# Turning the key-value sums of a linear attention: four TensorE transpositions and a copy, or one VectorE transposition and eight DMA moves

## The chip, the cores and the metric

The kernel runs on one core of a Trainium2 chip. A core has five engines that run their own instruction lists side by side: TensorE (PE in the profile, with its weight loads shown as PEld), VectorE (DVE), ScalarE (ACT), GpSimd (POOL) and SyncE (SP). SP computes nothing here; it issues DMAs, one after the other, and waits where a DMA has to wait. The metric is the device time of one execution in microseconds (us).

## The reference

Two branches are computed from the same input `x` (2048 rows of 512) and mixed row by row with a gate `g`:

```python
qkv = x @ wqkv                              # 32 heads of 16
pq, pk = q @ w_phi, k @ w_phi               # per head
phi = concat(softmax(p), softmax(-p))       # 32 features per head, for q and for k
kv = sum over rows s of phi_k[s]^T v[s]     # per head 32 x 16
z  = sum over rows s of phi_k[s]            # per head 32
a = (phi_q @ kv) / (phi_q . z + 1e-6) @ wo
b = mish(x @ w1 + b1) @ w2                  # 512 -> 1376 -> 512
out = g * a + (1 - g) * b,  g = sigmoid(x . gate_w)
```

`kv` is a sum over all 2048 rows, so no numerator `phi_q @ kv` can be made before the whole key pass is over.

## The kernel before, in words

The kernel has two passes. Pass A runs over eight chunks of 256 rows: it projects k, v and q (each fp32 product is made from three TensorE products of a high and a low part), turns k into features and adds `phi_k^T v` into one PSUM tile `kvp`, which lives through the whole pass. Pass B runs over four blocks of 512 rows: eleven steps `up0` to `up10` make the hidden columns of branch b, `dn0` to `dn10` multiply them by `w2`, and between them stand the q features, the numerators `nu0` and `nu1` (PE reads `kvb`, the turned kv sums, as weights, and `eT`, the turned q features, as the moving side), and the products `wo0` to `wo3` with `wo`.

The order of everything is written out by hand in the strings `FIRST` to `BLOCK`: each word names a step, `run` carries the steps out in that order, and `pin` keeps every instruction in it. So each engine's queue is the order of the words that give it work. A word with `+` belongs to the next stage.

The steps around the change:

- `km` is the last word of `LAST`, the last chunk of pass A. VectorE multiplies `kvp` by a mask of zeros and ones (`mask`, made by GpSimd at the start of the kernel at L193) and writes the result to an SBUF tile `km` (L455). `kvp` holds sums for pairs of heads, and the mask keeps only products of a head with itself.
- `@kt` stands in `BLOCK0` after `up3` and ahead of `dn1`. PE makes four 128x128 transpositions of `km` against the identity `ident` into a PSUM tile `kvT` (L460), and ScalarE copies that to `kvb` (issued at L461, recorded under the helper's line L121). `kvT` takes one of the three PSUM buffers of the tag `a`, which the `up` tiles use in turn.
- `mi3`, `hi3` and `lo3` follow `@kt` in the string: ScalarE's Mish of `up3`, its rounding `h`, and GpSimd's remainder `l` (L504).
- `gr` in `BLOCK0` sends the gate's row out and back (L531, L532), `lq3` loads q rows (L553), `mv0` and `mv1` move the turned q features to `eT` with sixteen DMAs each (L592). All of these are in SP's queue. `mv0` waits for `tr1`, a VectorE transposition (L572).
- `nu0` in `BLOCK0`, after `dn5`, is the first reader of `kvb` (L602, recorded under L101).

VectorE's transposition (the profile calls it STREAM_TRANSPOSE) turns each 32x32 block by itself: the blocks stay where they are.

Of the kernel before, what the change touches and what calls it, by code (L numbers as in the profile page):

```python
# [8 lines left out]

F32 = mybir.dt.float32  # L10
# [5 lines left out]
P = 128  # L16
# [5 lines left out]
NG = 4  # L22
SC = 256
# [37 lines left out]

BLOCK0 = """
    up0 mi0 hi0 lo0 gr lq3 S1 rS1 mx2 mn2 d02 d12 up1 @z mi1 hi1 lo1 T0 D0 m0 de0 rd0 sc0 es0 tr0 up2 mi2 hi2 lo2 dn0
    T1 D1 m1 de1 rd1 sc1 es1 tr1 mv0 lq0+ lq1+ mx3 mn3 d03 d13 up3 @kt mi3 hi3 lo3 dn1
    up4 mi4 hi4 lo4 WL0 dn2 E2 S2 T2 rS2 D2 m2 de2 rd2 sc2 es2 tr2 up5 mi5 hi5 lo5 WL1 dn3 E3 ge gg up6 mi6 hi6 lo6 dn4
    up7 mi7 hi7 lo7 dn5 nu0 oh0 S3 T3 rS3 ol0 D3 m3 de3 rd3 sc3 es3 tr3 mv1 up8 mi8 hi8 lo8 dn6
    mx0+ mn0+ d00+ d10+ mx1+ mn1+ d01+ d11+ lq2+ lq3+ wo0 ag0 wo1 ag1 E0+ E1+ S0+ T0+ rS0+ D0+ m0+ de0+ rd0+ sc0+ es0+ tr0+
# [22 lines left out]
def tile_gated_mix(ctx: ExitStack, tc: tile.TileContext, xT, wv, wkT, wqT, bd, w1a, w1b, b1, w2a, w2b, wo, out):  # L90
    nc = tc.nc
    const = ctx.enter_context(tc.tile_pool(name="const", bufs=1))
# [4 lines left out]
    pin = tc.keep_in_program_order  # L97
    V, G_, A_, Sy = nc.vector, nc.gpsimd, nc.scalar, nc.sync

    def mm(*a, **k):  # L100
        return pin(nc.tensor.matmul(*a, **k))  # L101

    def T(shape, dt, tag, bufs, name):
        nm[0] += 1
        return sp.tile(shape, dt, name=f"{name}_{nm[0]}", tag=tag, bufs=bufs)

    def k8(name, tag, dt=F32R):
        return T([P, 2048], dt, tag, 2 if tag in ("eT", "E") else 1, name)

    def k4(name, tag, dt=F32):  # L110
        return T([P, 1024], dt, tag, {"tx": 2, "oh": 2, "z": 1}[tag], name)

    def k2(name, tag, dt=F32):
        return T([P, 512], dt, tag, {"pq": 3, "io": 4, "hl": 8}[tag], name)

    def psum(name, tag, bufs={"a": 3, "dn": 4, "kv": 1}):
        nm[0] += 1
        return pp.tile([P, 512], F32, name=f"{name}_{nm[0]}", tag=tag, bufs=bufs[tag])

    def act(out_, in_, fn=AF.Copy, **k):  # L120
        return pin(A_.activation(out_, in_, fn, **k))  # L121
# [7 lines left out]
    def f32(ap):  # L129
        return ap.bitcast(F32)  # L130
# [52 lines left out]
    md = k2("md", "io")[:, :P].rearrange("p (h f) -> p h f", f=DH)  # L183
# [2 lines left out]
    pin(G_.affine_select(md, md, pattern=[[DH, 8], [0, DH]], compare_op=ALU.is_ge, fill=0.0, base=DH - 1, channel_multiplier=-1))  # L186
    b1s = const.tile([P, NF], F32, name="b1s")
    pin(G_.dma_start(b1s, b1))
    ident = const.tile([P, P], F32, name="ident")
    make_identity(nc, ident)  # L190
    mask = const.tile([P, 2, 2, 32], F32, name="mask")
    for a in range(2):
        pin(G_.tensor_add(mask[:, :, a, :], *[md[:, o : o + 4, :].rearrange("p (r h) f -> p r (h f)", r=2) for o in (0, 4)]))  # L193
    g_sb = const.tile([P, S // P], F32, name="g_sb")
    og_sb = const.tile([P, S // P], F32, name="og_sb")
    ge_sb = const.tile([P, S // P], F32, name="ge_sb")
    kvb = const.tile([P, NG, P], F32, name="kvb")


    steps = {}  # L200
# [1 line left out]
    def at(key, name, fn):  # L202
        steps.setdefault((key, name), []).append(fn)
# [11 lines left out]
    kvs = []  # L215
# [226 lines left out]
    B = {}  # L442

    def mid_ops():
        key = ("A", NCH - 1)

        def zh():
            B["zs"] = [k4("zs", "tx", F32R) for _ in range(2)]
            act(B["zs"][0], zacc)

        def km():
            B["km"] = k2("km", "io")
            shape = [P, NG, 2, 64]
            m = mask[:, :, :, :].rearrange("p r a f -> p r (a f)")[:, None, :, :].to_broadcast(shape)
            pin(V.tensor_mul(B["km"][:, :].rearrange("p (g r f) -> p g r f", g=NG, r=2), kvs[0][:, :, None, :].to_broadcast(shape), m))  # L455

        def kt_():
            pt = psum("kvT", "a")
            for G in range(NG):
                pin(nc.tensor.transpose(pt[:, G * P : (G + 1) * P], B["km"][:, G * P : (G + 1) * P], ident))  # L460
            act(kvb, pt[:, :].rearrange("p (g d) -> p g d", g=NG))  # L461

        def z():
            B["zb"] = k4("zb", "z")
            for a in range(2):
                ps = psum("z", "dn")
                for j in range(2):
                    mm(ps, onr, B["zs"][j][:, a * 512 : (a + 1) * 512], start=(j == 0), stop=(j == 1))
                act(B["zb"][:, a * 512 : (a + 1) * 512], ps)

        at(key, "zh", zh)
        at(key, "zl", lambda: pin(V.tensor_sub(B["zs"][1], zacc, f32(B["zs"][0]))))
        at(key, "km", km)
        at(("B", 0), "@kt", kt_)
        at(("B", 0), "@z", z)


    def b_ops(b):
# [68 lines left out]
        for t in range(4):  # L547
            d = {}
# [37 lines left out]
        for h in range(2):  # L586
            def mv(h=h):
                eTs[h] = k8("eT", "eT", F32)[:, :].rearrange("p (t q x) -> p t q x", t=2, q=4)
                for q in range(4):
                    for k in range(4):  # L590
                        o = 64 * (k % 2) + 32 * (k // 2)
                        pin(Sy.dma_start(eTs[h][o : o + 32, :, q, :], Ep[key, h][32 * q : 32 * q + 32, :, k * 256 : (k + 1) * 256]))  # L592

            def nu(h=h):
                ev = eTs[h][:, :, :, :].rearrange("p t q (b c) -> p b (t q) c", c=32)
                po = [psum("num", tag) for tag in (("a", "a") if b and h else ("kv", "a"))]
                for bh in range(2):
                    for c in range(4):
                        u = 4 * bh + c
                        for r in range(2):  # L600
                            o = (u % 2) * 64 + 32 * r
                            mm(po[r][32 * c : 32 * c + 32, bh * SC : (bh + 1) * SC], kvb[64 * r : 64 * r + 64, u // 2, o : o + 32], ev[64 * r : 64 * r + 64, u, :, :], start=True, stop=True, skip_group_check=True)  # L602
                for r in range(2):
                    num[h, r] = po[r]

            def oh(h=h):
                for gp in range(2):
                    ohl[h, gp] = k4("ohl", "oh", F32R)
                    act(ohl[h, gp][:, :512], num[h, gp])

            def ol(h=h):
                for gp in range(2):
                    pin(V.tensor_sub(ohl[h, gp][:, 512:], num[h, gp], f32(ohl[h, gp][:, :512])))

            at(key, f"mv{h}", mv)
            at(key, f"nu{h}", nu)
            at(key, f"oh{h}", oh)
            at(key, f"ol{h}", ol)
# [56 lines left out]
    x_ops(0, (("A", NCH - 2), "ldx", "ldw0"), ("A", NCH - 1))  # L675
    wo_ops()
    mid_ops()
    for b in range(NB):
        b_ops(b)
# [47 lines left out]
    for j in range(2):  # L727
        h, l = [w[:, 2 * j : 2 * j + 2, :].rearrange("p k f -> p (k f)") for w in (wvh, wvl)]
# [94 lines left out]
```

## Time and profile before

| what | value |
|---|---|
| median of 3 runs | 450.24 us (450.02 to 450.66) |
| the profiled execution | 449.89 us, of which 448.2 us span from its first to its last instruction |
| TensorE busy | 443.4 us, 99% of the span |
| VectorE busy | 307.6 us, 69% |
| ScalarE busy | 194.6 us, 43% |
| GpSimd busy | 164.7 us, 37% |
| mean granted TensorE clock | 0.999 of full speed |

The span is what the profile shows of the program; the rest of the profiled execution's time, 1.7 us, lies before and after it. All views are of that one execution. A row of the timeline gives the start in us from the span's start, the duration in us, the engine, the line of the kernel, the operation, the tiles written and read, the shape and the number of instructions merged into the row; in square brackets stands how long the engine stood idle before it, and what ended that. A row of the chain that ended last gives the start, how much of the span the piece takes up, and what it is. Matmul records overlap, because PE starts a matmul before the one ahead of it has drained; the distance between starts is what a matmul costs PE.

### The profile page before, as it was taken

How to read it: one execution, taken by the hardware profiler on the slowest of the kernel's cores; microseconds unless marked ns; L12 is line 12 of the kernel's file. 1: busy time of each engine (PE TensorE's matmuls, PEld its weight loads, DVE VectorE, ACT ScalarE, POOL GpSimd, SP SyncE). 2: the span in 40 equal slices, each digit the busy share in tenths (PEclk: the TensorE clock that was granted, in tenths of full speed). 3: DMA queues.
4: the chain of work that ended last, by engine and by line, in shares of the span. 5: the costliest groups of instructions: out<-in, count | busy, mean ns of one | idle time of the engine just before them, and what ended most of it. 6: DMA issues, size and time to landing. Idle time of an engine off the chain costs nothing.

```text
span 448.2 us, 7216 instructions
## 1 busy us (share of the span) xinstructions
PE 443.4 (99%) x2882; PEld 363.9 (81%) x2882; DVE 307.6 (69%) x411; ACT 194.6 (43%) x268; POOL 164.7 (37%) x102
## 2 busy tenths in 40 slices
PE   8999999999999999999999999999999999999996
PEld 7888888888888888878788878888878888887885
DVE  3798559459398999997979998369769329701103
ACT  3644533444335465627255352644262643242330
POOL 3448687677861445521122220214220222221121
PEclk9999999999999999999999999999999999999999
DMA  7721522614623100405243151321241302030002
GB/s 264 278 95 47 191 68 97 191 12 175 188 81 111 48 24 20 123 17 143 78 112 123 40 151 53 89 95 47 60 129 48 94 1 95 18 78 1 1 0 95
DMA packets 26026, 40.09 MB, mean 89 GB/s; under 512 B 5764, under 2 KB 14468, under 8 KB 25992
## 3 DMA queue, kind: packets, MB, share of 16 engines
q1 hardware_dynamic: 25672, 39.22, 28.6%
q8 instruction: 23, 0.38, 0.3%
q10 hardware_dynamic: 288, 0.39, 0.2%
q14 instruction: 11, 0.09, 0.1%
q0 software_dynamic: 32, 0.01, 0.0%
HBM read 22.82 MB, written 8.40 MB: 70 GB/s over the span
## 4 chain that ended last, share of the span: by engine, by line
PE 99%; ACT 0%; DVE 0%; issue 0%
PE proj L101 30%; PE up L101 27%; PE down L101 27%; PE wo L101 10%; PE kvp L101 2%; PE num L101 2%; PE fuse L101 1%; PE warm L101 1%; PE rest L101 0%; PE z L101 0%; ACT wkh L121 0%; DVE io L654 0%; PE kvT L460 0%; DVE ones L171 0%
## 5 line engine op out<-in xcount | busy, mean ns | idle before, releaser
L504 POOL TENSOR_TENSOR l<-act,h 128x512 fp32r<-128x512 f32 x44 | 63.9, 1453 | 218.0 <-ACT h L121 183.8
L121 ACT ACTIVATE act<-up,b1s 128x512 f32<-128x512 f32 x44 | 30.3, 689 | 92.2 <-PE up L101 91.3
L324 POOL TENSOR_TENSOR zacc<-zacc,E 128x1024 f32<-128x1024 f32 x16 | 39.8, 2486 | 43.9 <-DVE E L286 43.9
L121 ACT ACTIVATE E<-E 128x1024 f32<-128x1024 f32 x32 | 33.4, 1058 | 37.3 <-DVE E L271 37.2
L286 DVE TENSOR_TENSOR E<-E,Sm 128x1024 f32<-128x1024 f32 x32 | 46.5, 1453 | 1.1
L275 DVE TENSOR_REDUCE Sm<-E 128x64 f32<-128x1024 f32 x32 | 38.6, 1206 | 5.0 <-ACT E L121 5.0
L101 PE MATMUL wo<-woh,ohl 128*128 128x512 f32 x128 | 41.2, 389 | 0.0
L101 PE MATMUL down<-w2ah,h 128*128 128x512 f32 x96 | 37.7, 393 | 0.0
L101 PE MATMUL down<-w2al,h 128*128 128x512 f32 x96 | 37.4, 390 | 0.0
L101 PE MATMUL down<-w2ah,l 128*128 128x512 f32 x96 | 37.4, 389 | 0.0
L259 DVE TENSOR_REDUCE mx<-proj 128x32 f32<-128x512 f32 x16 | 11.0, 689 | 32.5 <-PE proj L101 32.5
L101 PE MATMUL down<-w2bh,h 128*128 128x512 f32 x78 | 30.6, 392 | 0.0
L101 PE MATMUL down<-w2bl,h 128*128 128x512 f32 x78 | 30.4, 390 | 0.0
L101 PE MATMUL down<-w2bh,l 128*128 128x512 f32 x78 | 30.3, 389 | 0.0
L409 DVE TENSOR_TENSOR xbl<-xraw,xbh 128x1024 fp32r<-128x1024 f32 x8 | 11.9, 1526 | 26.0 <-ACT xbh L121 26.0
L121 ACT ACTIVATE h<-act 128x512 fp32r<-128x512 f32 x44 | 27.8, 632 | 1.4
L101 PEld LDWEIGHTS wo<-woh,ohl 128*128 128x128 f32 x128 | 24.0, 188 | 5.0
L121 ACT ACT_TABLE_LOAD x19 | 24.4, 1283 | 5.5 <-PE up L101 5.2
L121 ACT ACTIVATE io<-wo,g_sb 128x512 f32<-128x512 f32 x16 | 10.9, 688 | 35.2 <-PE wo L101 35.2
L101 PE MATMUL up<-xbh,w1ah 128*128 128x512 f32 x96 | 25.8, 390 | 0.0
L101 PE MATMUL up<-xbl,w1ah 128*128 128x512 f32 x96 | 25.7, 389 | 0.0
L101 PE MATMUL up<-xbh,w1al 128*128 128x512 f32 x96 | 25.7, 389 | 0.0
(123 smaller groups left out, 968.9 us busy)
## 6 DMA issues: line engine op xcount, KB each, us to landing
eT<-E SPq DMA_DIRECT2D x128, 64.0 KB, 2.0
xraw<-in_xT_dram SPq DMA_DIRECT2D x15, 512.0 KB, 4.4
pqd<-qs SPq DMA_DIRECT2D x16, 256.0 KB, 3.3
pq<-pqd SPq DMA_DIRECT2D x16, 256.0 KB, 2.9
out_dram<-io SPq DMA_DIRECT2D x15, 256.0 KB, 2.4
raw<-in_w1a_dram SPq DMA_DIRECT2D x3, 512.0 KB, 5.1
raw<-in_w2a_dram SPq DMA_DIRECT2D x3, 512.0 KB, 3.8
wT<-in_wkT_dram SPq DMA_DIRECT2D x4, 256.0 KB, 4.3
```

Source lines behind the costliest of these rows:

```text
L101: return pin(nc.tensor.matmul(*a, **k))
L121: return pin(A_.activation(out_, in_, fn, **k))
L259: pin(V.tensor_reduce(d[name], hv(src()), axis=AX.X, op=op))
L275: pin(V.tensor_reduce(d["S"], hv(d["E"][:, :]), axis=AX.X, op=ALU.add))
L286: pin(eng.tensor_mul(hv(d["E"][:, :]), hv(d["E"][:, :]), d["S"][:, :, None].to_broadcast([P, 2 * H, DH])))
L324: at(key, f"z{t}", lambda d=d: pin(G_.tensor_add(zacc, zacc, d["E"])))
L409: pin(V.tensor_sub(xb[b][1][:, :, sl], kt(raw[h], SC), f32(xb[b][0][:, :, sl])))
L504: pin(G_.tensor_sub(U[i]["l"], U[i]["a"], f32(U[i]["h"])))
```

## The change

The change alters how `km` becomes `kvb`. The multiplication by the mask now writes 256 columns rather than 512: the blocks that belong to two different halves (`r`) of a group of heads were written as zeros before, and are not written now. VectorE then turns every 32x32 block of these 256 columns in place. Eight DMAs, all in SP's queue right behind, carry the blocks to the partitions where `nu` reads them: each takes 32 partitions of 4 runs of 32 numbers, 16 KB in all. The step `@kt`, with its four transpositions, its PSUM tile and its copy on ScalarE, is gone, and so is `ident`. The mask is now 32 columns wide and made by three additions instead of two. `kvb` holds 256 columns rather than 512, and `nu` reads from it the same numbers in weights of the same shape.

```diff
-    T1 D1 m1 de1 rd1 sc1 es1 tr1 mv0 lq0+ lq1+ mx3 mn3 d03 d13 up3 @kt mi3 hi3 lo3 dn1
+    T1 D1 m1 de1 rd1 sc1 es1 tr1 mv0 lq0+ lq1+ mx3 mn3 d03 d13 up3 mi3 hi3 lo3 dn1
...
-    ident = const.tile([P, P], F32, name="ident")
-    make_identity(nc, ident)
-    mask = const.tile([P, 2, 2, 32], F32, name="mask")
-    for a in range(2):
-        pin(G_.tensor_add(mask[:, :, a, :], *[md[:, o : o + 4, :].rearrange("p (r h) f -> p r (h f)", r=2) for o in (0, 4)]))
+    mask = const.tile([P, 32], F32, name="mask")
+    for o in (2, 4, 6):
+        pin(G_.tensor_add(mask, md[:, :2, :].rearrange("p h f -> p (h f)") if o == 2 else mask, md[:, o : o + 2, :].rearrange("p h f -> p (h f)")))
...
-    kvb = const.tile([P, NG, P], F32, name="kvb")
+    kvb = const.tile([P, 8, 32], F32, name="kvb")
...
             B["km"] = k2("km", "io")
-            shape = [P, NG, 2, 64]
-            m = mask[:, :, :, :].rearrange("p r a f -> p r (a f)")[:, None, :, :].to_broadcast(shape)
-            pin(V.tensor_mul(B["km"][:, :].rearrange("p (g r f) -> p g r f", g=NG, r=2), kvs[0][:, :, None, :].to_broadcast(shape), m))
-
-        def kt_():
-            pt = psum("kvT", "a")
-            for G in range(NG):
-                pin(nc.tensor.transpose(pt[:, G * P : (G + 1) * P], B["km"][:, G * P : (G + 1) * P], ident))
-            act(kvb, pt[:, :].rearrange("p (g d) -> p g d", g=NG))
+            m = B["km"][:, :256]
+            pin(V.tensor_mul(m.rearrange("p (n x) -> p n x", x=32), kvs[0].rearrange("p g (a x) -> p (g a) x", a=2), mask[:, None, :].to_broadcast([P, 8, 32])))
+            pin(V.transpose(m, m))
+            m = m.rearrange("p (g a x) -> p g a x", g=NG, a=2)
+            for e in range(2):
+                for r in range(2):
+                    for a in range(2):
+                        o, i = 64 * r + 32 * a, 64 * e + 32 * r
+                        pin(Sy.dma_start(kvb[o : o + 32, e::2, :], m[i : i + 32, :, a, :]))
...
-        at(("B", 0), "@kt", kt_)
...
-                            o = (u % 2) * 64 + 32 * r
-                            mm(po[r][32 * c : 32 * c + 32, bh * SC : (bh + 1) * SC], kvb[64 * r : 64 * r + 64, u // 2, o : o + 32], ev[64 * r : 64 * r + 64, u, :, :], start=True, stop=True, skip_group_check=True)
+                            mm(po[r][32 * c : 32 * c + 32, bh * SC : (bh + 1) * SC], kvb[64 * r : 64 * r + 64, u, :], ev[64 * r : 64 * r + 64, u, :, :], start=True, stop=True, skip_group_check=True)
```

The lists of instructions of the two kernels differ in nothing but these steps and the waits that go with them: on SP the eight moves stand ahead of the gate's row (L531); on ScalarE the Mish of `up3` takes over the wait for PE; on PE two `up` steps lose a wait for ScalarE, and the first `nu` gains waits for the eight moves.

More of the change, by code (lines that the diff above doesn't have):

```diff
@@ L6 @@
 from concourse import mybir
-from concourse.masks import make_identity
 from concourse._compat import with_exitstack
```

## The prediction

> **What bounds the kernel now.** I read the page's shares of busy time first, then the chain that ended last, then the list of who PE waited for, and last the timeline around the step that goes.
>
> ```profile
> span 448.2 us, 7216 instructions
> PE 443.4 (99%) x2882; PEld 363.9 (81%) x2882; DVE 307.6 (69%) x411; ACT 194.6 (43%) x268; POOL 164.7 (37%) x102
> PE 99%; ACT 0%; DVE 0%; issue 0%
> ```
>
> PE is busy for 99% of the span and is 99% of the chain. The list of waits has only these two for PE's matmuls:
>
> ```profile
> PE warm L101 <- DVE ones L171: 1.1, 1, 1.1
> PE proj L101 <- ACT wkh L121: 0.2, 1, 0.2
> ```
>
> Both belong to the first steps of the kernel. After them PE stands still for nobody. So an instruction taken from PE's list shortens the run by what it costs PE, if nobody is late for the earlier PE, and work put on other engines costs nothing while PE does not wait for it.
>
> **What goes from PE.** The chain around the four transpositions (start, share of the span, what), PE's timeline there, and two stretches of that timeline with the busy time of each engine:
>
> ```profile
> 163.31 2.72 PE up L101 x12
> 166.03 0.44 PE kvT L460 x4
> 166.47 2.77 PE down L101 x12
> 169.24 2.72 PE up L101 x12
> ```
> ```profile
> 165.87 0.60 PE L460 MATMUL kvT<-ident,km 128*128 128x128 f32 x4
> 166.22 0.48 PE L101 MATMUL down<-w2ah,h 128*128 128x512 f32 x1
> 166.54 0.40 PE L101 MATMUL down<-w2al,h 128*128 128x512 f32 x1
> 169.08 1.07 PE L101 MATMUL up<-xbh,w1ah 128*128 128x512 f32 x4
> ```
> ```profile
> 160.43:163.15 2.72, 2.72 (x14) 2.25 (x13) 2.72 (x6) 2.66 (x5) 1.05 (x2) 1.00 0.21 24
> 165.87:169.08 3.21, 3.21 (x18) 2.69 (x16) 3.00 (x7) 1.81 (x3) 0.97 (x2) 1.00 0.00 0
> ```
>
> The first stretch is `dn0`, twelve matmuls from the start of its first to the start of the next step: 2.72 us, 0.227 each. The second is the transpositions and `dn1`, also twelve matmuls: 3.21 us. The difference, 3.21 - 2.72 = 0.49 us, is what the four transpositions cost PE. Of it, 0.35 lies between the first transposition and the first `down` (165.87 to 166.22), 0.09 between that `down` and the next (0.32 where 0.227 is usual), 0.05 in the ten after it. The chain says the same: 0.44 and 2.77 - 2.72 = 0.05. From below, the 0.35 alone goes. From above the nearest row is one transposition's own duration, here the row of the line:
>
> ```profile
> L460 PE MATMUL kvT<-ident,km x4: 270/272/273, 165.9 to 166.2; 128*128 128x128 f32 x4
> ```
>
> Four of them end to end would be 4 x 0.272 = 1.09 us. I take 0.49, since the four starts lie within 0.35 us: they overlap.
>
> The Trainium skill, page TensorE: Matmul & The Clock Gate, section Part 4: PE-mode transpose, gives about 275 ns for a 128x128 transposition inside a kernel and says that such transpositions do not engage the full clock. By it, four would be an estimated 1.10 us and the sum 448.8 us. The row's 272 ns agrees with the duration, and the starts disagree with adding them up; the granted clock stays at 1.00 in the stretch.
>
> **What is added to VectorE.** The multiplication at 158.12, a like one of 256 columns, and the transposition of 1024 columns:
>
> ```profile
> 158.12 0.63 DVE L455 TENSOR_TENSOR km<-kvp,mask 128x512 f32<-128x512 f32 x1
> L706 DVE TENSOR_TENSOR xl<-xraw,xh 128x256 fp32r<-128x256 f32 x2 | 0.8, 424 | 0.1
> L572 DVE STREAM_TRANSPOSE E<-E 128x1024 f32<-128x1024 f32 x16 | 19.9, 1244 | 0.5
> ```
>
> The new multiplication takes 0.42 by the second row, the transposition 1.244 / 4 = 0.31 by the third. Against 0.63 that is 0.10 us more. From above, with both at the full price of the larger forms, it would be 1.24 us more; from below, should the multiplication scale to half, 0.31 + 0.31 - 0.63 = 0. I take 0.10, as the second row has the same shape. VectorE is busy without a gap here, so all that follows on it comes 0.10 later, `tr1` and with it `mv0` included. That lateness ends where VectorE waits for work that PE sets, in `BLOCK0`'s second half:
>
> ```profile
> 203.17 0.69 ACT L121 ACTIVATE io<-wo,g_sb 128x512 f32<-128x512 f32 x1 [2.03 <-PE wo L101]
> 206.26 1.22 DVE L275 TENSOR_REDUCE Sm<-E 128x64 f32<-128x1024 f32 x1 [2.62 <-ACT E L121]
> ```
>
> ScalarE waits for `wo`, then makes the exponential that VectorE has waited 2.62 us for. From here on the other engines move with PE, so PE's 0.49 us cannot be eaten up slowly over the later blocks.
>
> **What is added to SP.** Its timeline, the durations of a like move, and landing times:
>
> ```profile
> 148.24 5.56 SPq L314 DMA_DIRECT2D pqd<-qs  x2
> 159.75 0.30 SPq L531 DMA_DIRECT2D gd<-gr  x1
> 160.91 0.40 SPq L532 DMA_DIRECT2D ge_sb<-gd  x1
> 161.41 0.44 SPq L553 DMA_DIRECT2D pq<-pqd  x1
> 176.05 10.24 SPq L592 DMA_DIRECT2D eT<-E  x16
> ```
> ```profile
> L592 SPq DMA_DIRECT2D eT<-E x128: 586/595/1808, 176.1 to 400.0; - x128
> ```
> ```profile
> eT<-E SPq DMA_DIRECT2D x128, 64.0 KB, 2.0
> pq<-pqd SPq DMA_DIRECT2D x16, 256.0 KB, 2.9
> ```
>
> SP is free from 153.8. The first move waits for the transposition, which ends at 158.12 + 0.42 + 0.31 = 158.9. Eight moves at 0.595, the middle duration of `mv`'s moves from SBUF to SBUF, end at 163.7. Behind them stand the gate's row, its way back, and `lq3`; the three take from 159.75 to 161.85 now, 2.1 us, so SP is free at 165.8. By the longest of `mv`'s issues, 1.81, it would be free at 175.5. I take 0.595; the lower end changes nothing.
>
> Who waits behind them: `lq3` would start at 165.3 and land 2.9 later, at 168.2. Its reader is `mx3`; `mv0` needs SP; `nu0` needs `kvb` and `mv0`:
>
> ```profile
> 175.91 0.64 DVE L259 TENSOR_REDUCE mx<-pq 128x32 f32<-128x512 f32 x1
> 190.93 1.09 PE L101 MATMUL num<-eT,kvb 64*32 64x256 f32 x32
> 213.94 1.09 PE L101 MATMUL num<-eT,kvb 64*32 64x256 f32 x32
> 198.95 10.18 SPq L592 DMA_DIRECT2D eT<-E  x16
> ```
>
> `mx3` has 7.7 us to spare and `mv0`, which starts at 176.05, has 10.2. `kvb` has landed at 163.7 + 2.0 = 165.7, 24.7 us before `nu0` at 190.93 - 0.49 = 190.44. `mv0` ends its issues at 186.29 and has landed by 188.3, so `nu0` keeps 2.1 us, or 2.0 with VectorE's 0.10. For `nu1` the same sum is 213.94 - 0.49 - (209.13 + 2.0) = 2.3 us. All of it is hidden: 0.
>
> **The rest together.** ScalarE loses the copy and the wait ahead of it, and the Mish of `up3` starts when `up3` has drained (164.96 + 1.07 = 166.03 at the latest) instead of at 167.00. `dn1` comes 0.35 us earlier, and reads its `l` with its third matmul, at 165.87 + 2 x 0.227 = 166.32:
>
> ```profile
> 166.51 0.60 ACT L121 ACTIVATE kvb<-kvT 128x512 f32<-128x512 f32 x1 [3.19 <-PE kvT L460]
> 167.00 0.68 ACT L121 ACTIVATE act<-up,b1s 128x512 f32<-128x512 f32 x1
> 162.15 4.03 POOL L504 TENSOR_TENSOR l<-act,h 128x512 fp32r<-128x512 f32 x2 [1.67 <-ACT h L121]
> 163.90 2.29 POOL L504 TENSOR_TENSOR l<-act,h 128x512 fp32r<-128x512 f32 x1
> 14.00 2.46 POOL L730 TENSOR_TENSOR wvl<-raw,wvh 128x1024 fp32r<-128x1024 f32 x1 [9.68 <-ACT wvh L121]
> ```
>
> The first two rows are ScalarE's copy and Mish, the others GpSimd's; of its two remainders the second starts at 163.90, so `dn1`'s was done about then, 2.4 us ahead. At the kernel's start GpSimd loses the identity and gains one addition, before an idle time of 9.68 us: 0. `nu` loads the same numbers in the same shape: 0.
>
> **The sum.** -0.49 + 0 = -0.49 us. The profiled execution took 449.89 us, span 448.2: it becomes 449.40, span 447.7. The median of the runs is 0.35 above the profiled execution, 450.24, and becomes 449.75, 0.11% less. What a measurement of this kernel can tell from no change is about 0.2%, 0.9 us (the three runs lie 0.64 apart), so the forecast is a gain too small to be told: 449.8.
>
> **Rivals.**
>
> - The transpositions cost PE their full duration, 1.09 us. For it: the 272 ns of each row; the overlap is read from starts alone, and matmul ends are modelled. Against it: the next matmul starts 0.35 after the first transposition, and nothing later on PE is late. Time: 450.24 - 1.09 = 449.15, 0.24% faster.
> - The saving is eaten: PE, 0.49 earlier, meets work that PE doesn't set, and waits for it. For it: `BLOCK0` leans on VectorE, which is full from 158 to 204. Against it: the spare times worked out above, 2.0 us at the least. Time: 450.24, no change.
> - The moves hold SP up so long that `mv0` is late and PE waits at `nu0`. SP is free at 158.9 + 8t + 2.1 for moves of t each; `mv0` is late from t = 1.88, PE waits once that lateness is over 2.0, at t = 2.13, and the kernel becomes slower by over 0.9 us at t = 2.30 (a wait of 1.4, less the 0.49 saved). For it: these moves have four short runs per partition, and no row of the trace has such a move. Against it: 0.595 is the middle, and even the longest, 1.81, is under the first bound. With t = 2.5 SP is free at 181.0, PE waits 181.0 - 176.05 - 2.0 = 2.95, and the time is 450.24 + 2.95 - 0.49 = 452.7.
>
> **How the numbers follow.** The forecast 0.66; the full duration 0.19; the eaten saving 0.07; the late `mv0`, with whatever else makes PE wait, 0.08. The runs' own spread moves the forecast's 449.75 by some 0.3 either way, which puts 0.03 of it on the faster side, and adds 0.02 to slower from what I do not see. So faster 0.22, same 0.68, slower 0.10. The range goes from the full duration less that spread, 448.8, to the eaten saving with it, 450.6; the slow rival lies outside.
>
> **What would show it.** Right: no L460 rows, `dn1` starting 0.227 after `up3`'s last matmul and taking 2.72, no new wait of PE in the list, span 447.7; eight moves on SP of about 0.6 each from 159, `lq3` issued near 165, `mv0` still starting near 176; VectorE's new pair near 0.42 and 0.31. Wrong: a wait of PE at `nu0` (SP or VectorE late), moves over 2 us each, or a saving near 1.1.

## The result, and the profile after

The changed kernel is slower. Its median is 451.15 us (450.45 to 452.36, 10 runs) against 449.88 us for the kernel before (449.11 to 451.21, 10 runs); the ratio is 1.0029, with a 95% interval from 1.0019 to 1.0039. The forecast was 449.8 us with a range from 448.8 to 450.6, and no measurable change. The profiled execution took 450.91 us, span 449.1.

The parts of the page that answer to those of before, and the list of PE's longest waits:

```profile
span 449.1 us, 7215 instructions
PE 442.4 (99%) x2878; PEld 362.6 (81%) x2878; DVE 311.7 (69%) x412; ACT 194.1 (43%) x267; POOL 162.2 (36%) x101
PE 86%; DVE 9%; SPq 2%; DMA 2%; issue 1%
```
```profile
PE warm L100 <- DVE ones L170: 1.1, 1, 1.1
PE num L100 <- DMA eT<-E: 1.0, 1, 1.0
```

PE's busy time fell by 1.0 us, but the chain no longer runs through PE alone, and there is a new wait: `nu0` waits for `mv0`'s moves. The timeline of PE and SP around it:

```profile
191.39 1.59 PE L100 MATMUL num<-eT,kvb 64*32 64x256 f32 x32 [0.95 <-DMA eT<-E]
192.91 1.21 PE L100 MATMUL up<-xbh,w1bh 128*128 128x512 f32 x4
...
158.87 5.16 SPq L459 DMA_DIRECT2D kvb<-km  x8
165.89 0.49 SPq L550 DMA_DIRECT2D pq<-pqd  x1
180.27 10.18 SPq L589 DMA_DIRECT2D eT<-E  x16
```

`mv0` starts at 180.27 and not at 176.05, 4.22 us late, though SP is free from 166.4. Two stretches, from `up2`'s first matmul to the first one behind `nu0`, say what PE lost. The first row is the kernel before, the second the changed one:

```profile
157.71:191.96 34.25, 34.25 (x182) 27.72 (x180) 33.46 (x43) 19.90 (x28) 18.66 (x10) 1.00 0.21 54
```
```profile
157.63:192.91 35.28, 34.33 (x178) 27.47 (x176) 34.52 (x39) 19.25 (x26) 15.65 (x10) 1.00 0.20 51
```

The stretch is 1.03 us longer. If the transpositions' 0.49 us went as forecast, PE waits 1.03 + 0.49 = 1.52 us at and inside `nu0`; that it went is shown further down, by a run of the changed kernel in which PE does not wait. The span grew by 0.9, so the rest of the kernel takes next to no part in it.

Why `mv0` is late stands in VectorE's timeline. Its rows in the changed kernel that differ in length from those before, with GpSimd's rows of the same time:

```profile
158.00 0.36 DVE L452 TENSOR_TENSOR km<-kvp,mask 128x256 f32<-128x256 f32 x1
158.40 0.45 DVE L453 STREAM_TRANSPOSE km<-km 128x256 f32<-128x256 f32 x1
158.77 1.18 DVE L272 TENSOR_REDUCE Sm<-E 128x64 f32<-128x1024 f32 x1
162.18 1.78 DVE L268 TENSOR_TENSOR E<-mn,pq 128x512 f32<-128x512 f32 x1
167.74 1.17 DVE L562 SCALAR_TENSOR_TENSOR den<-Dn 128x32 f32<-128x32 f32 x1
174.49 2.30 DVE L575 TENSOR_TENSOR Dn<-Dn,Sm 128x64 f32<-128x64 f32 x1
```
```profile
162.04 3.07 POOL L501 TENSOR_TENSOR l<-act,h 128x512 fp32r<-128x512 f32 x2 [1.67 <-ACT h L120]
167.48 1.38 POOL L501 TENSOR_TENSOR l<-act,h 128x512 fp32r<-128x512 f32 x1 [2.37 <-ACT h L120]
172.97 1.39 POOL L501 TENSOR_TENSOR l<-act,h 128x512 fp32r<-128x512 f32 x1 [4.12 <-ACT h L120]
174.32 2.39 POOL L430 TENSOR_TENSOR wol<-raw,woh 128x1024 fp32r<-128x1024 f32 x1
```

Three of these VectorE operations are longer than in the kernel before, where they take 0.69 us (shown further down), 0.19 and 0.23:

```profile
166.58 0.19 DVE L565 SCALAR_TENSOR_TENSOR den<-Dn 128x32 f32<-128x32 f32 x1
172.35 0.23 DVE L578 TENSOR_TENSOR Dn<-Dn,Sm 128x64 f32<-128x64 f32 x1
```

Each of the three starts while a GpSimd operation runs and ends less than its own usual length after it. The first starts at 162.18 and ends at 163.96; GpSimd's remainder of `up1`, the first of the two in its row, runs from 162.04 for 1.38 us, to 163.42. The second, a tiny one, starts at 167.74 and ends at 168.91, when GpSimd's has ended at 168.86. The third starts at 174.49 and ends at 176.79; GpSimd's ends at 176.71. Against the kernel before they take 1.78 - 0.69 = 1.09, 1.17 - 0.19 = 0.98 and 2.30 - 0.23 = 2.07 us more, together 4.14; the pair of multiplication and transposition takes 0.77 us between starts (158.00 to 158.77) instead of 0.54, 0.23 more. That is 4.37 us, less the 0.12 us by which this execution was ahead at 158: 4.25, which is the 4.22 of `mv0`.

In the kernel before, VectorE came first. VectorE and GpSimd, at two of the three places:

```profile
162.10 0.69 DVE L271 TENSOR_TENSOR E<-mn,pq 128x512 f32<-128x512 f32 x1
173.49 1.22 DVE L286 TENSOR_TENSOR E<-E,Sm 128x1024 f32<-128x1024 f32 x1
```
```profile
162.15 1.80 POOL L504 TENSOR_TENSOR l<-act,h 128x512 fp32r<-128x512 f32 x1 [1.67 <-ACT h L121]
173.54 2.33 POOL L504 TENSOR_TENSOR l<-act,h 128x512 fp32r<-128x512 f32 x1 [3.71 <-ACT h L121]
```

VectorE was first by 0.05 us both times, kept its usual length, and GpSimd took 1.80 and 2.33 us for what takes 1.3 alone. VectorE is not spared everything there: the multiplication by `zb` that follows the subtraction (the row `T<-E,zb`) waits in both kernels alike (2.33 and 2.31 us, where 1.18 is usual), so it adds nothing to the difference. So the theory to test: two of these operations exclude each other, whoever starts first makes the other wait to its end, and the change turned the order round.

### The profile page after: what moved, and what is told of

It is laid out like the page before. It is cut to its first block, busy times and chain, and to the rows that moved or that the text cites. A ratio compares the mean times of both kernels' runs of the same rounds, so it can differ in the third digit from the quotient of the medians.

```text
span 449.1 us, 7215 instructions
## 1 busy us (share of the span) xinstructions
PE 442.4 (99%) x2878; PEld 362.6 (81%) x2878; DVE 311.7 (69%) x412; ACT 194.1 (43%) x267; POOL 162.2 (36%) x101
## 4 chain that ended last, share of the span: by engine, by line
PE 86%; DVE 9%; SPq 2%; DMA 2%; issue 1%
PE proj L100 27%; PE down L100 23%; PE up L100 22%; PE wo L100 10%; SPq L589 2%; PE num L100 2%; PE kvp L100 2%; DMA wT<-in_wkT_dram 1%; DVE xbl L406 1%; DVE Sm L272 1%; PE fuse L100 1%; DVE E L283 1%; DVE T L554 1%; DVE E L268 1%; DVE Dn L575 1%
## 5 line engine op out<-in xcount | busy, mean ns | idle before, releaser
L501 POOL TENSOR_TENSOR l<-act,h 128x512 fp32r<-128x512 f32 x44 | 62.7, 1427 | 221.3 <-ACT h L120 202.1
L283 DVE TENSOR_TENSOR E<-E,Sm 128x1024 f32<-128x1024 f32 x32 | 45.6, 1425 | 1.1
```

The costliest lines, as they stand in the source:

```text
L283: pin(eng.tensor_mul(hv(d["E"][:, :]), hv(d["E"][:, :]), d["S"][:, :, None].to_broadcast([P, 2 * H, DH])))
L501: pin(G_.tensor_sub(U[i]["l"], U[i]["a"], f32(U[i]["h"])))
```

## The experiments

Theory A is that one: the order of VectorE and GpSimd flips, through VectorE's 0.23 us. Theory B is that the eight moves and their traffic slow VectorE, which would fit as well: they run from 158.9 to 164. Theory C is that GpSimd being earlier (PE and ScalarE have less to do ahead of `up3`'s remainder) is enough alone. All ratios are against the kernel before on the same chip, with 95% intervals.

**VectorE's lateness alone.** The kernel before with two small transpositions that undo each other:

```diff
             pin(V.tensor_mul(B["km"][:, :].rearrange("p (g r f) -> p g r f", g=NG, r=2), kvs[0][:, :, None, :].to_broadcast(shape), m))
+            for _ in range(2):
+                pin(V.transpose(B["km"][:, :32], B["km"][:, :32]))
```

> The kernel before, with two more VectorE transpositions of 32 columns of km, in place, right behind the multiplication by the mask (the second undoes the first); PE, ScalarE, SP and GpSimd keep their lists. It makes VectorE about 0.25 us later, as the change does (0.23). Theory A (GpSimd and VectorE shut each other out of SBUF: whoever starts first makes the other wait to its end; the change makes VectorE 0.2 us late, so that GpSimd's remainder of up1 starts first): the second feature subtraction at 162.1 takes about 1.8 us instead of 0.69, and tr1 ends over 1.2 us late, up to 5; PE's wait at nu0 is that lateness less about 3 us (2.7 to spare plus the transpositions, which stay on PE here), so 450 to 452 us. Theory B (the eight moves and their traffic slow VectorE): no moves, so VectorE is 0.25 late and no more, 449.9 us as before.

Measured: 451.15 us, ratio 1.0028 (1.0018 to 1.0038): the whole loss, with no moves and with the four transpositions still on PE. The row of the subtraction, of a later tiny operation and of `mv0`:

```profile
161.85 1.80 DVE L271 TENSOR_TENSOR E<-mn,pq 128x512 f32<-128x512 f32 x1
174.26 2.27 DVE L567 SCALAR_TENSOR_TENSOR den<-Dn 128x32 f32<-128x32 f32 x1
179.79 10.25 SPq L594 DMA_DIRECT2D eT<-E  x16
```

A holds and B is not needed. The lateness given here is twice the change's 0.23, so this run shows that lateness alone suffices, not that 0.23 us of it do. One size was off: the two small transpositions made VectorE 0.50 us later, not 0.25 (157.40 to 158.44 between the multiplication and the sum, 1.04 instead of 0.54), which matters below.

**Everything but the moves.** The changed kernel with its blocks written and turned straight in `kvb`:

```diff
-            m = B["km"][:, :256]
+            m = kvb[:, :, :].rearrange("p n x -> p (n x)")
...
-            m = m.rearrange("p (g a x) -> p g a x", g=NG, a=2)
-            for e in range(2):
-                for r in range(2):
-                    for a in range(2):
-                        o, i = 64 * r + 32 * a, 64 * e + 32 * r
-                        pin(Sy.dma_start(kvb[o : o + 32, e::2, :], m[i : i + 32, :, a, :]))
```

> The changed kernel without its eight moves: VectorE writes and turns the blocks where nu reads its weights, so the numerators are made from blocks that lie on wrong partitions. Theory A: nothing of the loss goes, the subtraction at 162.2 takes 1.8 us, mv0 starts near 180, 451.2 us. Theory B: the subtraction is back at 0.69 us, mv0 starts near 176, 449.4 us.

Measured: 450.66 us, ratio 1.0023 (1.0012 to 1.0035). The subtraction still takes 1.78 us and `mv0` starts at 179.96. From `up2` to behind `nu0` PE takes 35.36 us here and 35.28 with the moves. The moves cost nothing that can be told: B falls.

**Everything but the transposition on VectorE.** The changed kernel without this line:

```diff
-            pin(V.transpose(m, m))
```

> The changed kernel without VectorE's transposition; the eight moves stay, so nu reads blocks that are not turned. VectorE is 0.14 us earlier than in the kernel before (0.40 instead of 0.54 between the starts of the multiplication and the sum behind it). Theory A: the subtraction starts ahead of GpSimd again and takes 0.69 us; mv0 starts near 176, unless GpSimd's earlier remainder of up3 meets VectorE at 167.4 (theory C: then VectorE still loses 1 us or more there); 449.4 us by A, 450 to 451 by C. Theory B: 451.2, as the moves are there.

Measured: 449.48 us, ratio 0.9994 (0.9981 to 1.0007). The subtraction is back at its usual length, `mv0` starts at 176.93, and PE waits for nothing at `nu0`. The moves are all there. VectorE's multiplication of 256 columns alone, 0.40 us between starts, leaves VectorE 0.14 us ahead of the kernel before, and that is enough. Not every order is kept, though. GpSimd's remainder of `up4` comes first here, and VectorE's long multiplication waits 1.01 us for it (2.24 instead of 1.23):

```profile
173.34 2.24 DVE L283 TENSOR_TENSOR E<-E,Sm 128x1024 f32<-128x1024 f32 x1
173.22 1.29 POOL L500 TENSOR_TENSOR l<-act,h 128x512 fp32r<-128x512 f32 x1 [3.53 <-ACT h L120]
```

One such loss is less than what `nu0` has to spare, so PE does not see it.

**Only what leaves PE and ScalarE.** The kernel before without `@kt`:

```diff
-    T1 D1 m1 de1 rd1 sc1 es1 tr1 mv0 lq0+ lq1+ mx3 mn3 d03 d13 up3 @kt mi3 hi3 lo3 dn1
+    T1 D1 m1 de1 rd1 sc1 es1 tr1 mv0 lq0+ lq1+ mx3 mn3 d03 d13 up3 mi3 hi3 lo3 dn1
...
-            pin(V.tensor_mul(B["km"][:, :].rearrange("p (g r f) -> p g r f", g=NG, r=2), kvs[0][:, :, None, :].to_broadcast(shape), m))
+            pin(V.tensor_mul(kvb[:, :, :].rearrange("p g (r f) -> p g r f", r=2), kvs[0][:, :, None, :].to_broadcast(shape), m))
```

> The kernel before without the four transpositions and the copy: the masked product is written where nu reads its weights, so the numerators are made from sums that were not turned. VectorE and SP keep their lists; PE loses 0.49 us and ScalarE's Mish of up3 starts about 0.95 us earlier, so GpSimd's remainder of up3 does too. If VectorE's 0.2 us is the root (theory A), the subtraction at 162.1 stays at 0.69 us, VectorE stays on time up to there, and the run takes 449.4 us. If GpSimd's earlier remainder of up3 alone is enough (theory C), VectorE loses 1 us or more at 167.5, and more at 174, and the run takes 450 to 451.2. Theory B: 449.4.

Measured: 451.26 us, ratio 1.0025 (1.0015 to 1.0035): slower, though nothing was added anywhere and PE and ScalarE have less to do. VectorE and GpSimd:

```profile
173.66 1.20 DVE L568 TENSOR_TENSOR Sm<-Sm,den 128x64 f32<-128x64 f32 x1
174.90 3.33 DVE L286 TENSOR_TENSOR E<-E,Sm 128x1024 f32<-128x1024 f32 x1
```
```profile
173.49 1.29 POOL L503 TENSOR_TENSOR l<-act,h 128x512 fp32r<-128x512 f32 x1 [3.23 <-ACT h L121]
174.74 2.40 POOL L433 TENSOR_TENSOR wol<-raw,woh 128x1024 fp32r<-128x1024 f32 x1
```

The subtraction at 162 was in time here. At 173.5 PE's 0.49 us had moved GpSimd's remainder of `up4` ahead of VectorE: the small multiplication (0.23 us usually) waited 0.97 us for it, and the long one (1.23) 2.1 us for the remainder of `wo` that was next in GpSimd's queue. `mv0` starts at 179.57, and PE loses the time inside the numerators, which take 1.47 us (`nu0`, at 190.88) and 1.70 us (`nu1`, at 214.40) where each takes 1.09. So A's root is one of two: either half of the change flips an order and loses the time by itself. Theory C is right as well, with the place moved: the flip came at `up4`'s remainder, not at `up3`'s.

**GpSimd's long pieces moved away.** The changed kernel with the two remainders of `wo` two steps later:

```diff
-    up4 mi4 hi4 lo4 WL0 dn2 E2 S2 T2 rS2 D2 m2 de2 rd2 sc2 es2 tr2 up5 mi5 hi5 lo5 WL1 dn3 E3 ge gg up6 mi6 hi6 lo6 dn4
-    up7 mi7 hi7 lo7 dn5 nu0 oh0 S3 T3 rS3 ol0 D3 m3 de3 rd3 sc3 es3 tr3 mv1 up8 mi8 hi8 lo8 dn6
+    up4 mi4 hi4 lo4 dn2 E2 S2 T2 rS2 D2 m2 de2 rd2 sc2 es2 tr2 up5 mi5 hi5 lo5 dn3 E3 ge gg up6 mi6 hi6 lo6 WL0 dn4
+    up7 mi7 hi7 lo7 WL1 dn5 nu0 oh0 S3 T3 rS3 ol0 D3 m3 de3 rd3 sc3 es3 tr3 mv1 up8 mi8 hi8 lo8 dn6
```

> The changed kernel with GpSimd's two remainders of wo (2.4 us each) two steps later in its queue, behind the remainders of up6 and up7. Theory A: the losses at 162.2 (1.10 us) and 167.7 (0.98) stay, the 2.07 us at 174.5, where VectorE waited for the first of these two, goes or shrinks to what the remainder of up4 leaves; mv0 starts near 178.2, which is within nu0's 2.7 us to spare, so PE keeps its 0.49: 449.4 us, if the two pieces do not meet VectorE as badly at 186 to 190 (then nu1 is late, up to 451). Another theory in which the loss at 174.5 only follows from the earlier lateness: 451.1 as before.

Measured: 451.32 us, ratio 1.0041 (1.0025 to 1.0056, 4 runs). The first half went as A has it: the wait at 174.5 is gone and `mv0` starts at 178.18, where 178.2 was expected, and PE does not wait at `nu0`. But the two pieces met VectorE again, and PE waits later:

```profile
186.79 2.40 POOL L430 TENSOR_TENSOR wol<-raw,woh 128x1024 fp32r<-128x1024 f32 x1
187.30 1.98 DVE L566 TENSOR_TENSOR Sm<-Sm,den 128x64 f32<-128x64 f32 x1
189.31 2.34 DVE L283 TENSOR_TENSOR E<-E,Sm 128x1024 f32<-128x1024 f32 x1
197.67 0.50 PE L100 MATMUL wo<-woh,ohl 128*128 128x512 f32 x1 [0.56 <-DVE ohl L609]
214.22 1.77 PE L100 MATMUL num<-eT,kvb 64*32 64x256 f32 x32
```

`wo0` waits 0.56 us for VectorE, and `nu1` takes 1.77 us where it takes 1.09. The expectation allowed for that with up to 451; it became 451.3.

**Making GpSimd later, not VectorE earlier.** If the order is all, more work on ScalarE that delays GpSimd's remainders must bring the time back. First on the kernel with VectorE's lateness alone:

```diff
         def hi(i):
             U[i]["h"] = k2("h", "hl", F32R)
+            if b == 0 and i in (1, 4):
+                act(U[i]["a"][:, :P], U[i]["a"][:, :P])
             act(U[i]["h"], U[i]["a"])
```

> The last run but with VectorE's 0.25 us alone (the kernel before and the two small transpositions), and in addition ScalarE copies 128 columns of the Mish result onto itself ahead of the rounding of up1 and of up4, which makes GpSimd's remainders of these two steps about 0.3 us later; PE's and VectorE's lists stay. More work, nothing less. Theory A (who starts first shuts the other out; in the kernel before VectorE comes first by 0.05 us at 162.1 and again by 0.05 at 173.5): VectorE is first again at both places, the subtraction at 162 takes 0.69 us, mv0 starts 0.2 to 0.3 us later than in the kernel before and not 4, PE does not wait at nu0, 449.8 us. If the 0.25 us cost by themselves, through anything but the order of the two engines, the run stays at 451.1.

Measured: 451.47 us, ratio 1.0038 (1.0025 to 1.0052, 4 runs): a miss. VectorE's subtraction started at 162.41 and GpSimd's remainder at 162.33, still 0.08 us first, since VectorE was 0.50 us late and the copies gave only 0.35. So the copies were made longer, 512 columns:

```diff
-                act(U[i]["a"][:, :P], U[i]["a"][:, :P])
+                act(U[i]["a"], U[i]["a"])
```

> The kernel before with the two small transpositions, and ScalarE's copy onto itself ahead of the rounding of up1 and up4 now over all 512 columns, about 0.65 us. In the last two runs the two transpositions made VectorE not 0.25 but 0.50 us later (1.04 us from the multiplication to the sum behind it, where 0.54 stood), so the 0.35 us of the shorter copies did not put VectorE first. Theory A: GpSimd's remainder of up1 now starts near 162.6, VectorE's subtraction at 162.4 is first and takes 0.69 us; likewise at 173.8; mv0 starts within 0.7 us of the kernel before, PE does not wait, 449.9 us. If 0.5 us on VectorE cost by themselves: 451.2.

Measured: 449.67 us, ratio 1.0003 (0.9994 to 1.0012). The subtraction at 162.50 takes 0.69 us, GpSimd comes at 162.75, `mv0` starts at 176.44. VectorE is as late as in the run that lost 0.28%, and ScalarE has more to do.

The same for the kernel without `@kt`, with the copy ahead of `up4`'s rounding alone (`i in (4,)`):

> The kernel before without the four transpositions and the copy (sums not turned, as in the run without them), and ScalarE copies the Mish result of up4 onto itself ahead of its rounding, 0.65 us. Without that copy GpSimd's remainder of up4 started 0.17 us ahead of VectorE's small multiplication, VectorE waited 0.97 and, behind the remainder of wo, 2.1 more. Theory A: now the remainder starts about 0.65 later, VectorE's long multiplication is first, mv0 starts near 176.5 and PE keeps its 0.49: 449.4 us. Otherwise 451.2.

Measured: 449.37 us, ratio 0.9999 (0.9984 to 1.0014); the long multiplication takes 1.23 us again. And for the changed kernel itself, with the copy ahead of `up1`, `up3` and `up4` (`i in (1, 3, 4)`):

> The changed kernel with ScalarE's copy of 512 columns onto itself ahead of the rounding of up1, up3 and up4 of the first block: 2 us more work on ScalarE, nothing less on any engine; the result is the reference's. Theory A: GpSimd's remainders come 0.65 us later, VectorE is first at 162.2, 167.6 and 173.6, the 4.15 us of its waits go, mv0 starts near 176.3, PE does not wait and keeps 0.49 us: 449.4 us, as fast as without the transposition and faster than the changed kernel by 0.3%. If the loss has another root: 451.2 or more.

Measured: 449.53 us, ratio 0.9996 (0.9985 to 1.0007), so 0.33% better than the changed kernel's ratio. VectorE and SP:

```profile
162.52 0.69 DVE L268 TENSOR_TENSOR E<-mn,pq 128x512 f32<-128x512 f32 x1
159.22 5.16 SPq L459 DMA_DIRECT2D kvb<-km  x8
176.47 10.18 SPq L591 DMA_DIRECT2D eT<-E  x16
```

All three long operations are short again, the eight moves are there, and adding 2 us of work to ScalarE made the changed kernel faster. Three kernels that had lost the time, by VectorE's lateness, by GpSimd's being early and by both, got it back when GpSimd was made later. That settles the order as the cause. In this run and the one before it PE's 0.49 us should show as a ratio of 0.9989; both intervals hold that and also no change. The trace tells it better than the times do. From `up2`'s first matmul to the first one behind `nu0`, where the kernel before takes 34.25 us, this run takes

```profile
157.94:191.70 33.76, 33.76 (x178) 27.34 (x176) 32.94 (x44) 21.32 (x30) 18.54 (x10) 1.00 0.23 59
```

and PE is busy throughout: 0.49 us less, as forecast. The run before it takes 33.76 us as well.

**A version that keeps the saving.** The mask's multiplication moved to ScalarE, which has 1.9 us free at 153.5 and can scale each partition by its own number. For that the last sums of `kvp` (`kv`) are moved ahead of `E1+` and `zl`:

```diff
+        def kc():
+            B["km"] = k2("km", "io")
+            src, dst = kvs[0].rearrange("p g (a x) -> p (g a) x", a=2), B["km"][:, :256].rearrange("p (n x) -> p n x", x=32)
+            for h in range(2):
+                act(dst[:, :, 16 * h : 16 * h + 16], src[:, :, 16 * h : 16 * h + 16], scale=mask[:, 16 * h : 16 * h + 1])
...
-            pin(V.tensor_mul(m.rearrange("p (n x) -> p n x", x=32), kvs[0].rearrange("p g (a x) -> p (g a) x", a=2), mask[:, None, :].to_broadcast([P, 8, 32])))
             pin(V.transpose(m, m))
...
-    v1 ve1 lq2+ mx1+ mn1+ d01+ d11+ q0 WH0 qe0 st0 q1 WH1 zh qe1 st1 E1+ zl kv S0+ rS0+ km
+    v1 ve1 lq2+ mx1+ mn1+ d01+ d11+ q0 WH0 qe0 st0 q1 WH1 zh qe1 st1 kv kc E1+ zl S0+ rS0+ km
```

> The changed kernel with the mask's multiplication on ScalarE: two copies from PSUM with a scale per partition, in an idle time of 1.9 us at 153.5, so VectorE is left with the transposition alone, 0.37 us between starts instead of 0.77 (0.54 in the kernel before). The result is the reference's. Theory A: VectorE is 0.17 us earlier than in the kernel before, comes first at 162 and at 173 as without the transposition, PE keeps its 0.49 us: 449.3 us, 0.1% under the kernel before. If the order at 173 flips all the same, as without the transpositions on PE alone: 450.5 to 451.2.

Measured: 449.15 us (11 runs), ratio 0.9986 (0.9978 to 0.9995): faster than both kernels. Its rows:

```profile
152.85 0.62 ACT L120 ACTIVATE km<-kvp,mask 128x128 f32<-128x128 f32 x2
157.62 0.39 DVE L457 STREAM_TRANSPOSE km<-km 128x256 f32<-128x256 f32 x1
161.33 0.68 DVE L268 TENSOR_TENSOR E<-mn,pq 128x512 f32<-128x512 f32 x1
176.30 10.18 SPq L594 DMA_DIRECT2D eT<-E  x16
```

VectorE is left with the transposition, 0.31 us between starts, and `mv0` stays in time: `nu0` does not wait, and the stretch from `up2` to behind it takes 33.76 us. One part of the expectation missed. The order at 173 did flip, which was to cost 450.5 to 451.2 us:

```profile
172.70 2.25 DVE L283 TENSOR_TENSOR E<-E,Sm 128x1024 f32<-128x1024 f32 x1
172.58 1.29 POOL L506 TENSOR_TENSOR l<-act,h 128x512 fp32r<-128x512 f32 x1 [3.54 <-ACT h L120]
173.83 3.40 POOL L430 TENSOR_TENSOR wol<-raw,woh 128x1024 fp32r<-128x1024 f32 x1
```

It cost VectorE 1.02 us and no more, because here the long multiplication was the one that waited, and it came ahead of the remainder of `wo`, which took 3.40 us instead of 2.40. In the kernel without `@kt` the small multiplication waited, the remainder of `wo` slipped in behind it, and the long one waited again. So what a flip costs depends on what VectorE is about to start when it comes, and PE waits only when the losses add up to more than `nu0` has to spare (2.7 us, worked out below).

## Why the prediction was wrong, point by point

- **PE's bound and its saving: right.** `dn1` follows `up3` with no gap and no L460 row is left. With ScalarE's copies, where PE does not wait, the changed kernel's stretch is 33.76 us instead of 34.25, the 0.49 us that was forecast; so the 35.28 us without the copies hold 35.28 - 33.76 = 1.52 us of waits. The rival that had the full duration of 1.09 us is out, and with it the sum that followed from adding up durations.
- **SP and the moves: right.** They took 5.16 us for eight, 0.645 each where 0.595 was taken; `lq3` was issued at 165.89 instead of 165.3; without the moves the loss stays. The rival's place, `nu0` behind a late `mv0`, was right, its mechanism was not: SP was idle from 166.4 to 180.27.
- **What is added to VectorE: this step failed.** The term itself was near (0.23 us between starts; 0.10 was forecast), but the sentence that all that follows comes 0.10 later, and the upper bound of 1.24, took VectorE's durations for fixed. With fixed durations even 1.24 us would have stayed inside the 2.0 us to spare. They are not fixed: 0.2 us of lateness became 4.2, because three operations behind it came second to GpSimd's. The wait at `nu0` with VectorE late is among the signs that the prediction itself listed for being wrong.
- **The rest together: this step failed too.** That the Mish of `up3`, and GpSimd behind it, start earlier was costed at 0: the prediction asked only whether `dn1` finds its inputs in time. But an earlier GpSimd operation can take the place of a VectorE one, and the kernel without `@kt` lost 0.25% by that alone. The argument that an engine off PE's path may be early for nothing was the flaw; the saving carried its own loss. The rival "the saving is eaten" is nearest to this, PE's earliness meeting VectorE's work; it capped the loss at the 0.49 us saved, since it too held VectorE's times fixed.
- **The spare time at `nu0`** was 2.7 us rather than 2.0: landing counts from the start of an issue, and the prediction added it to the end of the last one. The lateness of 4.22 passes 2.7 by the 1.52 us that PE waited. The kernel without `@kt` bears the 2.7 out: there `mv0` starts 21.42 us behind `up2`'s first matmul, 3.08 later than the 18.34 of the kernel before, and the stretch to behind `nu0` takes 34.13 us, 0.37 over the 33.76 without waits. With these two terms the sum closes: -0.49 + 1.52 = 1.03 us, inside what the runs say (1.0019 to 1.0039 of 449.88 us is 0.85 to 1.75 us).

The signs were in the trace of before: one form had two durations. The multiplication by `zb` took 2.33 us at 162.71 and 1.18 at 169.88; GpSimd's remainder took 1.80 and 2.29 at 162 and 164, 1.30 at 159.19 and 1.29 at 180.26. The 2.29 stands in a row that the prediction shows. The Trainium skill states the rule, on the page SBUF — State Buffer, section Who interferes with whom: a VectorE instruction with two inputs in SBUF and a GpSimd instruction that reads SBUF contend for one shared pair of ports, the one that issues first holds it for its whole length, and the order of issue decides who is blocked. The trace agrees, in both directions: 0.19 us became 1.17 on VectorE, 1.3 became 2.33 on GpSimd. The prediction did not draw on it.

## What to carry to other kernels

Where one form of instruction has two durations in a trace, ask who was running when the long ones started; if two engines exclude each other, their durations depend on order, and a margin of 0.05 us can hide microseconds. Before an engine's work is called free because it is off the path, look at what each engine gets in front of when it becomes earlier or later, and count slack in the order of such pairs, not only in time. A gain on the bound engine shifts all that follows it against the others, so it can lose more than it saves; a small delay at the right place, or moving work off the crowded engine, brings it back.

## What the runs showed of the hardware that was not expected

- A tiny VectorE operation pays the whole rest of a GpSimd one: 0.23 us became 2.30 (128x64, at 174.49), behind one of 2.39 us.
- Not all VectorE operations wait. In the changed kernel a sum over 1024 columns ran from 173.24 in 1.22 us, and a transposition of 1024 columns in the run with the later pieces from 191.69 in 1.25, both their usual lengths, while GpSimd's multi-input operations ran beside them. One input is no safe sign: in the same run an addition of a number to 128x4 (`ge_sb`, 0.13 us in the kernel before) took 1.09 from 192.86 and ended at 193.95, when GpSimd's remainder of `wo` had ended at 193.92.
- A VectorE transposition of 128x256 took 0.39 to 0.45 us, and two of 128x32 in a row made VectorE 0.50 us later. In proportion to the 1.25 us of 1024 columns those two would be an estimated 0.08: a small transposition costs far more than its columns.
